# Moving what TensorE waits for ahead in the queues at each change of stage of the first batch

## The chip, the core and the metric

The kernel runs on one core of a Trainium2 chip. The core has TensorE (PE, matrix products into PSUM), VectorE (DVE), ScalarE (ACT), GpSimd (POOL) and SyncE (SP), which here issues the transfers. Each engine works through its own instructions in the order of the program, and waits at an instruction until what it needs is there. The metric is the time of one execution on the device in microseconds (us), a median of several.

## The reference

There are two blocks. The first is a long convolution by Fourier transform over 12480 positions, for 4 batches and 128 channels, with a filter that a small network makes from embeddings of the positions. The second is a gated layer over all 49920 tokens.

```python
h_filt = (np.maximum(pos_emb @ w1, 0.0) @ w2) * np.exp(-0.01 * pos)[:, None]
u = x * v
y = irfft(rfft(u, n=2 * S, axis=1) * rfft(h_filt, n=2 * S, axis=0), n=2 * S, axis=1)[:, :S, :]
a = (x * y).reshape(B * S, D)          # B, S, D = 4, 12480, 128
h = a @ w_in                           # w_in 128 x 2048
out = (h * np.cos(h)) @ w_out          # w_out 2048 x 128
```

## The kernel before

The transform is done in two steps of 96 and 120 points, as matrix products. The stages of the first batch have the names F1 (first step forward), F2 (second step forward, and the product with the filter's spectrum), I1 (first step back) and I2 (second step back). The filter goes through its own F1 just ahead of the first batch's F1, and F2 takes the filter and the first batch together (`f2_both_units`). With I2 the gated layer begins, and the later batches run between its matmuls until the end.

The program is written with generators: one `next` puts a small piece of work into the queues. `units` runs a stage: `before` puts in what a unit needs, `mm` its matmuls, `after` what empties its PSUM banks, one unit later. Beside F1 and I1 other work is strewn in by `beside`: the conversion of the gated layer's weights, which arrive as 64-bit numbers, in eight pieces a matrix (`convert_units`), and six groups of twiddled rows for I2 (`some_groups`). There are eight PSUM banks in these stages. A tile of a pool with `bufs=2` shares two buffers with its namesakes: a third one gets its buffer when all that uses the first one is done, its store too.

```python
    def convert_units(pool, pieces):
        raws, half = [], None
        for i in range(len(pieces) + 1):
            while len(raws) < min(i + 2, len(pieces)):
                raws.append(pool.tile([P, WCOL, 2], U32, name="raw", bufs=3))
                nc.sync.dma_start(raws[-1][:, :, :], pieces[len(raws) - 1][1])
            yield
            if i > 0:
                float32_join(pieces[i - 1][0], raws[i - 1], *half)
            if i < len(pieces):
                half = float32_parts(pool, raws[i])
...  # class Tables, def sines: for each output, one multiply-add chain on the engine, then:
                self.waiting.append((dst, t, TWO_PI / turn))
                yield
                if len(self.waiting) == self.lag:
                    self.finish(1)
        def finish(self, n):
            for _ in range(n):
                dst, t, scale = self.waiting.pop(0)
                nc.scalar.activation(dst, t, AF.Sin, scale=scale)
...  # def inverse_tables, after ten such outputs, with lag 4, on GpSimd:
        t.finish(len(t.waiting))
        for kept, made in ((csd, cs), (rowsd, rows), (twd, tw_t)):
            nc.sync.dma_start(kept[:, :, :], made[:, :, :])
...  # def turn, called by make_w for w and by make_t for tm:
        nc.scalar.activation(term, first, AF.Copy, scale=one)
        if spare is None:
            nc.vector.scalar_tensor_tensor(out=dst, in0=second, scalar=other, in1=term,
                                           op0=ALU.mult, op1=ALU.add)
        else:
            nc.scalar.activation(spare, second, AF.Copy, scale=other)
            nc.gpsimd.tensor_tensor(dst, term, spare, op=ALU.add)
...
    def f1_evict(ps, b, share):
        copy, negated = f1_takers(b, share)
        pj = ps[:, 0:4 * N1].rearrange("p (i r k) -> p r k i", i=2, r=2)
        copy(out=parts[0:ODD, :, :, b, :], in_=pj[0:ODD])
        yield
        copy(out=parts[ODD:KE, 0, :, b, :], in_=pj[ODD:KE, 1])
        negated(parts[ODD:KE, 1, :, b, :], pj[ODD:KE, 0])
        yield
...
    def f2_product(pool, ps, h, k1, whole):
        y = parts[0:N2, :, k1:k1 + 2, :, :].rearrange("p r k b i -> p r b (k i)")
        t = pool.tile([N2, 2, CB, 4], F32, name="t", bufs=1 + whole)
        uu = ps[0:N2, :].rearrange("p (r b j) -> p r b j", r=2, j=4)
        if whole:
            for r, (dst, hh) in enumerate(((y, h[:, :, :, :]), (t[:, :, :, :], h[:, ::-1, :, :]))):
                u = uu[:, r]
                twice = bass.AP(tensor=u.tensor, offset=u.offset,
                                ap=[u.ap[0], [0, 2], *u.ap[1:]])
                nc.vector.tensor_tensor(dst, twice, hh, op=ALU.mult)
                yield
        for r, op in ((0, ALU.subtract), (1, ALU.add)):
            if not whole:
                nc.vector.tensor_tensor(y[:, r], uu[:, 0], h[:, r], op=ALU.mult)
                yield
                nc.vector.tensor_tensor(t[:, r], uu[:, 1], h[:, 1 - r], op=ALU.mult)
            nc.gpsimd.tensor_tensor(y[:, r], y[:, r], t[:, r], op=op)
            yield
...
    def i1_evict(pool, ps, b):
        pj = ps[0:N1, 0:4 * N2].rearrange("p (i r j) -> p r j i", i=2, r=2)
        other = pool.tile([N1, N2, 2], F32, name="other")
        nc.scalar.copy(out=other[:, :, :], in_=pj[:, 1])
        for h, op in ((0, ALU.add), (1, ALU.subtract)):
            nc.vector.tensor_tensor(slots[0:N1, b, h * N2:(h + 1) * N2, :], pj[:, 0],
                                    other[:, :, :], op=op)
            yield
...
    def units(n, steps, before, mm, after, parts, ahead=2):
        for j in range(min(ahead, n)):
            for _ in before(j) or ():
                pass
        yield 0.0
        last = iter(())
        for j in range(n):
            early = iter(before(j + ahead) or () if j + ahead < n else ())
            now = None
            for i in range(parts):
                if i == 0 or 2 * i == max(parts, 2):
                    now = mm(j, now, min(i, 1))
                if i == 0 and parts == 1:
                    now = mm(j, now, 1)
                next(last, None)
                next(early, None)
                yield steps / parts
            for _ in early:
                pass
            next(last, None)
            last = after(j, now)
        for _ in last:
            pass
        yield REST
...
    def f2_both_units(bank):
        with tc.tile_pool(name="both", bufs=2) as pool:
            ws = {}
            def before(j):
                ws[j] = pool.tile([KE, 2, N2], F32, name="w")
                for i in range(2):
                    make_w(ws[j][:, i, :], 2 * j + i, half=bank)
                nc.sync.dma_start(wd[j, :, :, :], ws[j][:, :, :])
            def mm(j, ps, i):
                if i == 0:
                    ps = bank(), bank()
                for filt in range(2):
                    f2_mm(ps[filt], ws[j], 2 * j, i, filt=filt == 1)
                return ps
            def after(j, ps):
                h = pool.tile([N2, 2, CB, 4], F32, name="h", bufs=3)
                nc.scalar.activation(h[:, :, :, :].rearrange("p r b j -> p (r b j)"),
                                     ps[1][0:N2, :], AF.Copy, scale=1.0 / M)
                nc.sync.dma_start(hd[j, :, :, :, :], h[:, :, :, :])
                yield from f2_product(pool, ps[0], h, 2 * j, True)
            yield from units(N1 // 2, F2_STEPS, before, mm, after, 4, ahead=1)
...
    def some_groups(pool):
        for g in SOME:
            t = pool.tile([N1, G, 2, R], F32, name="some", bufs=2)
            yield from make_group(pool, g, t, G, bufs=2)
        next(backs[0])
...  # the main program
            f1 = f1_units(bank, ftile[0:FR, :, :, :], 0.53, f1_evict_filter)
            for _ in first_u:
                for _ in range(2):
                    next(f1)
            keep.__exit__(None, None, None)
            with tc.tile_pool(name="tables", bufs=1) as pool:
                sines = inverse_tables(pool)
                for i, _ in enumerate(f1):
                    if i % 5 == 0:
                        next(sines, None)
                for _ in sines:
                    pass
            backs = [inverse_units(lambda: bank(), b) for b in range(B)]
            def beside(units, pieces, more=lambda pool: iter(())):
                with tc.tile_pool(name="convert", bufs=1) as pool:
                    convert, other = convert_units(pool, pieces), more(pool)
                    for i, _ in enumerate(units):
                        if i % 14 == 0:
                            next(convert, None)
                        elif i % 5 == 0:
                            next(other, None)
                    for _ in [*convert, *other]:
                        pass
            beside(f1_units(bank, slots[0:R, :, :, :], 0.55),
                   [(wind[:, c], w) for c, w in in_pieces])
            lpool = ctx.enter_context(tc.tile_pool(name="late", bufs=1))
            cs = third_table(lpool)
            nc.sync.dma_start(cs[:, :, :], csd[:, :, :])
            for _ in f2_both_units(bank):
                pass
            first.close()
...
            w_in_sb = wpool.tile([D, DFF], F32, name="w_in_sb")
            w_out_sb = wpool.tile([P, NFC, D], F32, name="w_out_sb")
            quarter = wpool.tile([P, 1], F32, name="quarter")
            nc.vector.memset(quarter[:, :], 0.25)
            nc.sync.dma_start(w_in_sb[:, :], wind[:, :])
            beside(i1_units(bank), [(w_out_sb[:, c, :], w) for c, w in out_pieces], some_groups)
```

## Time and profile before

The three runs took 3785.52, 3782.50 and 3784.62 us, median 3784.62 us. The profiled execution has a span of 3782.9 us. Times of stretches and of single instructions count from the start of that span.

| engine | busy us | share of the span |
|---|---|---|
| TensorE matmuls (PE) | 3701.9 | 98% |
| TensorE weight loads (PEld) | 2107.3 | 56% |
| VectorE (DVE) | 2762.4 | 73% |
| GpSimd (POOL) | 2592.6 | 69% |
| ScalarE (ACT) | 2520.3 | 67% |

The stages that the change touches lie in the first 350 us:

| stage of the first batch | first matmul at us | last matmul begins, or group ends, at us |
|---|---|---|
| F1 of the filter | 63.2 | 112.7 |
| F1 | 112.7 | 164.8 |
| F2 | 169.5 | 267.7 |
| I1 | 271.0 | 331.7 |
| I2 | 336.6 | into the gated layer |

How to read the lines below: `L404` is line 404 of the kernel; `ps<-c,slots` gives the tiles written and read; `x14` is a number of instructions. An idle time has behind `<-` the engine, tile and line whose end is thought to have ended it. A matmul of 32-bit numbers stands as two instructions. The granted clock is TensorE's, as a share of full speed. In the chain, each step is followed back to what released it.

### The profile page before, as it was taken

The numbers are of one execution on the slowest core, as the hardware profiler recorded it, in microseconds if no ns is written. First come the engines' busy times: TensorE is split into PE (matmuls) and PEld (weight loads), VectorE is DVE, ScalarE is ACT, GpSimd is POOL, SyncE is SP. The second block draws the span as 40 slices with busy tenths as digits, with TensorE's granted clock in tenths as the row PEclk, the third lists the DMA queues.
The fourth block names the chain that finished last, engine by engine and source line by source line (L and its number), as shares of the span: only waits on it lengthen the run. The fifth ranks groups of instructions, "written<-read, shape, count | busy, mean of one in ns | idle before, by whom it ended". The sixth has DMA issues, their size and how long they took to land.

```text
span 3782.9 us, 47199 instructions
## 1 busy us (share of the span) xinstructions
PE 3701.9 (98%) x13546; PEld 2107.3 (56%) x13546; DVE 2762.4 (73%) x5562; ACT 2520.3 (67%) x4683; POOL 2592.6 (69%) x2342
## 2 busy tenths in 40 slices
PE   7898999999999999999999999999999999999999
PEld 6777555655466555555565556555566544444444
DVE  7887887688866777778766786788765566666666
ACT  5756776766665557666665567666664677777777
POOL 7667886588854665688745664788644577777776
PEclk9999999999999999999999999999999999999999
DMA  5263552022202650122103540122105200000000
GB/s 166 69 179 106 149 147 57 18 70 79 74 18 67 179 159 27 33 78 78 57 18 110 173 127 18 51 78 76 41 12 167 87 20 20 17 21 20 17 22 13
DMA packets 209498, 276.14 MB, mean 73 GB/s; under 512 B 17111, under 2 KB 146535, under 8 KB 209111
## 3 DMA queue, kind: packets, MB, share of 16 engines
q1 hardware_dynamic: 209239, 273.12, 24.7%
q8 instruction: 109, 1.79, 0.2%
q14 instruction: 150, 1.23, 0.1%
HBM read 193.64 MB, written 79.42 MB: 72 GB/s over the span
## 4 chain that ended last, share of the span: by engine, by line
PE 83%; POOL 6%; DVE 3%; DMA 3%; ACT 2%; issue 2%; SPq 0%; POOLq 0%; DVEq 0%; ACTq 0%
PE ph L737 32%; PE acc L762 27%; PE cv L762 5%; PE cv L501 4%; PE cv L476 4%; POOL f L746 4%; PE cv L404 3%; PE cv L445 3%; PE ph L126 2%; DMA hd<-h 2%; PE ps L404 1%; POOL tm L297 1%; DMA tm<-td 1%; DVE k L743 1%; ACT cs L751 1%
## 5 line engine op out<-in xcount | busy, mean ns | idle before, releaser
L746 POOL TENSOR_TENSOR f<-a,k 128x512 f32<-128x512 f32 (+1 forms) x1568 | 1987.4, 1268 | 1054.2 <-DVE k L743 1052.0
L737 PE MATMUL ph<-at,w_in_sb 128*128 128x512 f32 (+1 forms) x3136 | 1600.2, 592 | 5.8 <-DVE gt L753 5.2
L740 ACT ACTIVATE a<-ph,quarter 128x512 f32<-128x512 f32 (+1 forms) x1568 | 1073.4, 685 | 760.5 <-PE ph L737 751.0
L762 PE MATMUL acc<-gt,w_out_sb 128*128 128x512 f32 (+1 forms) x2688 | 1374.1, 593 | 9.7 <-ACT ot L768 9.3
L753 DVE TENSOR_TENSOR gt<-ph,cs 128x512 f32<-128x512 f32 (+1 forms) x1568 | 1077.3, 687 | 318.5 <-ACT cs L751 288.9
L743 DVE TENSOR_SCALAR k<-a 128x512 f32<-128x512 f32 (+1 forms) x1568 | 768.5, 490 | 623.4 <-ACT a L740 601.6
L751 ACT ACTIVATE cs<-f 128x512 f32<-128x512 f32 (+1 forms) x1568 | 980.3, 625 | 330.6 <-POOL f L746 328.1
L762 PEld LDWEIGHTS acc<-gt,w_out_sb 128*128 128x128 f32 x2688 | 505.6, 189 | 662.8 <-issue 619.5
L737 PEld LDWEIGHTS ph<-at,w_in_sb 128*128 128x128 f32 x3136 | 554.0, 190 | 338.7 <-issue 269.5
L471 POOL TENSOR_TENSOR slots<-slots,t 120x256 f32<-120x256 f32 x384 | 311.4, 817 | 58.7 <-DVE t L464 26.0
L501 PEld LDWEIGHTS cv<-slots,tm 96*104 96x104 f32 x1920 | 241.0, 171 | 110.7 <-issue 83.0
L501 PE MATMUL cv<-slots,tm 96*104 96x128 f32 x1920 | 255.6, 275 | 10.4 <-DVE tm L293 4.9
L762 PE MATMUL cv<-gt,w_out_sb 128*128 128x512 f32 (+1 forms) x448 | 224.5, 583 | 0.7 <-DVE gt L753 0.7
L476 PEld LDWEIGHTS cv<-cs,slots 120*96 120x96 f32 x1536 | 176.7, 167 | 67.6 <-issue 65.7
L476 PE MATMUL cv<-cs,slots 120*96 120x120 f32 x1536 | 183.1, 266 | 0.0
L445 PE MATMUL cv<-slots,w 124*120 124x256 f32 x576 | 173.0, 380 | 0.0
L445 PEld LDWEIGHTS cv<-slots,w 124*120 124x120 f32 x576 | 103.6, 184 | 123.8 <-issue 111.1
L404 PEld LDWEIGHTS cv<-c,slots 104*124 104x124 f32 x768 | 132.5, 192 | 71.2 <-issue 58.3
L404 PE MATMUL cv<-c,slots 104*124 104x192 f32 x768 | 151.2, 326 | 4.8 <-DVE gt L753 3.5
L762 PEld LDWEIGHTS cv<-gt,w_out_sb 128*128 128x128 f32 x448 | 84.9, 190 | 104.5 <-issue 99.5
L392 DVE TENSOR_TENSOR xt<-xt,vt 104x256 f32<-104x256 f32 x177 | 138.3, 788 | 0.4 <-DMA vt<-in_v_dram 0.4
L486 DVE TENSOR_TENSOR slots<-cv,other 96x240 f32<-96x240 f32 x384 | 133.7, 394 | 4.2 <-ACT other L484 4.2
(129 smaller groups left out, 2564.1 us busy)
## 6 DMA issues: line engine op xcount, KB each, us to landing
h<-hd SPq DMA_DIRECT2D x144, 240.0 KB
tm<-td SPq DMA_DIRECT2D x96, 312.0 KB
xt<-in_x_dram SPq DMA_DIRECT2D x120, 208.0 KB
vt<-in_v_dram SPq DMA_DIRECT2D x120, 208.0 KB
xs<-in_x_dram SPq DMA_DIRECT2D x120, 208.0 KB
zd<-zs SPq DMA_DIRECT2D x119, 208.0 KB
zb<-zd SPq DMA_DIRECT2D x96, 256.0 KB
w<-wd SPq DMA_DIRECT2D x144, 116.2 KB
```

The costliest lines, as they stand in the source:

```text
L404: nc.tensor.matmul(ps[0:KE, i * 2 * N1:(i + 1) * 2 * N1], u[:, b, 0:KE, i], c1[0:u.shape[0], :, :].rearrange("p r k -> p (r k)"), start=Tr ...
L445: nc.tensor.matmul(pi, w[:, i, :], parts[0:KE, :, k], start=True, stop=True)
L471: nc.gpsimd.tensor_tensor(y[:, r], y[:, r], t[:, r], op=op)
L476: nc.tensor.matmul(ps[0:N1, (i * 2 + r) * N2:(i * 2 + r + 1) * N2], parts[0:N2, r, :, b, i], cs[:, r, :], start=True, stop=True)
L501: nc.tensor.matmul(ps[0:R, i * D:(i + 1) * D], t[:, i, r, :], slots[0:N1, :, place, :], start=(r == 0), stop=(r == 1))
L737: nc.tensor.matmul(ph[:, 0:m], w_in_sb[:, c * P:(c + 1) * P], ats[n][:, 0:m], start=True, stop=True)
L740: nc.scalar.activation(a[:, 0:m], ph[:, 0:m], AF.Identity, bias=quarter[:, 0:1], scale=INV_TWO_PI)
L743: nc.vector.tensor_scalar(out=k[:, 0:m], in0=a[:, 0:m], scalar1=ROUND, scalar2=ROUND, op0=ALU.add, op1=ALU.subtract)
L746: nc.gpsimd.tensor_tensor(f[:, 0:m], a[:, 0:m], k[:, 0:m], op=ALU.subtract)
L751: nc.scalar.activation(cs[:, 0:m], f[:, 0:m], AF.Sin, scale=TWO_PI)
L753: nc.vector.tensor_tensor(gt[:, 0:m], ph[:, 0:m], cs[:, 0:m], op=ALU.mult)
L762: nc.tensor.matmul(accs[n][:, 0:m], w_out_sb[:, c, :], gt[:, 0:m], start=(c == 0), stop=(c == NFC - 1))
```

## The change

At each change of stage of the first batch, what TensorE waits for is put ahead in the queues:

- tables: the last four sines no longer come as one block; they are strewn one by one between the evictions, and the first batch's F1 starts among them;
- first matrices: the first pair of twiddled matrices `w` of F2 is made at the start of F1 and not after it; its pool moves out of F2's pool for that, and the stores of `w` now come after the store of `h` of the unit, those of the first ones after the first `h`;
- last sums: the two last sums of F2's product go to VectorE in place of GpSimd;
- conversions: the pieces come every 11th step in F1 and every 10th in I1 (before: every 14th), the groups for I2 at every fourth step (before: every fifth);
- transfers and groups: the first group of I2 with its transfers is put in ahead of the last group of `some_groups`, not after everything.

No arithmetic is added or left out.

```diff
--- before.py
+++ after.py
@@ -1,5 +1,6 @@
 import math
 from contextlib import ExitStack
+from itertools import chain
 
 import concourse.bass as bass
 import concourse.tile as tile
@@ -265,7 +266,9 @@
                            [(rows[:, i, :], q) for i, q in enumerate((0, 1, 2, 3))])
         yield from t.sines(mid, part4, TURN, [(tw_t[:, 0, :], 1), (tw_t[:, 1, :], 0)],
                            eighths=slice(H - 1, N2, H))
-        t.finish(len(t.waiting))
+        while t.waiting:
+            t.finish(1)
+            yield
         for kept, made in ((csd, cs), (rowsd, rows), (twd, tw_t)):
             nc.sync.dma_start(kept[:, :, :], made[:, :, :])
 
@@ -450,7 +453,7 @@
             for r, src in enumerate((ftile[0:KE, :, k, :], above[0:KE, :, k - KF, :])):
                 nc.tensor.matmul(pi[:, r], w[:, i, :], src, start=True, stop=True)
 
-    def f2_product(pool, ps, h, k1, whole):
+    def f2_product(pool, ps, h, k1, whole, sums=nc.gpsimd):
 
 
         y = parts[0:N2, :, k1:k1 + 2, :, :].rearrange("p r k b i -> p r b (k i)")
@@ -468,7 +471,7 @@
                 nc.vector.tensor_tensor(y[:, r], uu[:, 0], h[:, r], op=ALU.mult)
                 yield
                 nc.vector.tensor_tensor(t[:, r], uu[:, 1], h[:, 1 - r], op=ALU.mult)
-            nc.gpsimd.tensor_tensor(y[:, r], y[:, r], t[:, r], op=op)
+            sums.tensor_tensor(y[:, r], y[:, r], t[:, r], op=op)
             yield
 
     def i1_mm(ps, b, i):
@@ -601,32 +604,38 @@
             yield from units(N1 // 2, F2_STEPS, before, mm,
                              lambda j, ps: f2_product(pool, ps, hs.pop(j), 2 * j, False), 4)
 
-    def f2_both_units(bank):
-
+    def f2_both_units(bank, w_pool):
+
+        ws, unkept = {}, []
+
+        def before(j):
+            ws[j] = w_pool.tile([KE, 2, N2], F32, name="w")
+            for i in range(2):
+                make_w(ws[j][:, i, :], 2 * j + i, half=bank)
+            unkept.append(j)
+
+        def mm(j, ps, i):
+            if i == 0:
+                ps = bank(), bank()
+            for filt in range(2):
+                f2_mm(ps[filt], ws[j], 2 * j, i, filt=filt == 1)
+            return ps
+
+        def after(j, ps):
+            h = pool.tile([N2, 2, CB, 4], F32, name="h", bufs=3)
+            nc.scalar.activation(h[:, :, :, :].rearrange("p r b j -> p (r b j)"),
+                                 ps[1][0:N2, :], AF.Copy, scale=1.0 / M)
+            nc.sync.dma_start(hd[j, :, :, :, :], h[:, :, :, :])
+            while unkept:
+                k = unkept.pop(0)
+                nc.sync.dma_start(wd[k, :, :, :], ws[k][:, :, :])
+            yield from f2_product(pool, ps[0], h, 2 * j, True,
+                                  nc.vector if 2 * j + 2 == N1 else nc.gpsimd)
+
+        steps = units(N1 // 2, F2_STEPS, before, mm, after, 4, ahead=1)
+        yield next(steps)
         with tc.tile_pool(name="both", bufs=2) as pool:
-            ws = {}
-
-            def before(j):
-                ws[j] = pool.tile([KE, 2, N2], F32, name="w")
-                for i in range(2):
-                    make_w(ws[j][:, i, :], 2 * j + i, half=bank)
-                nc.sync.dma_start(wd[j, :, :, :], ws[j][:, :, :])
-
-            def mm(j, ps, i):
-                if i == 0:
-                    ps = bank(), bank()
-                for filt in range(2):
-                    f2_mm(ps[filt], ws[j], 2 * j, i, filt=filt == 1)
-                return ps
-
-            def after(j, ps):
-                h = pool.tile([N2, 2, CB, 4], F32, name="h", bufs=3)
-                nc.scalar.activation(h[:, :, :, :].rearrange("p r b j -> p (r b j)"),
-                                     ps[1][0:N2, :], AF.Copy, scale=1.0 / M)
-                nc.sync.dma_start(hd[j, :, :, :, :], h[:, :, :, :])
-                yield from f2_product(pool, ps[0], h, 2 * j, True)
-
-            yield from units(N1 // 2, F2_STEPS, before, mm, after, 4, ahead=1)
+            yield from steps
 
     def i1_units(bank):
         with tc.tile_pool(name="mid", bufs=2) as pool:
@@ -654,7 +663,8 @@
         for g in SOME:
             t = pool.tile([N1, G, 2, R], F32, name="some", bufs=2)
             yield from make_group(pool, g, t, G, bufs=2)
-        next(backs[0])
+            if g == SOME[-2]:
+                next(backs[0])
 
     def i2_units(bank, b, bufs):
 
@@ -857,33 +867,34 @@
             keep.__exit__(None, None, None)
             with tc.tile_pool(name="tables", bufs=1) as pool:
                 sines = inverse_tables(pool)
-                for i, _ in enumerate(f1):
-                    if i % 5 == 0:
-                        next(sines, None)
-                for _ in sines:
-                    pass
+                first_f1 = f1_units(bank, slots[0:R, :, :, :], 0.55)
+                for i, _ in enumerate(chain(f1, first_f1)):
+                    if i % 5 == 0 and next(sines, "made") == "made":
+                        break
 
 
 
             backs = [inverse_units(lambda: bank(), b) for b in range(B)]
 
-            def beside(units, pieces, more=lambda pool: iter(())):
+            def beside(units, pieces, every, more=lambda pool: iter(())):
                 with tc.tile_pool(name="convert", bufs=1) as pool:
                     convert, other = convert_units(pool, pieces), more(pool)
                     for i, _ in enumerate(units):
-                        if i % 14 == 0:
+                        if i % every == 0:
                             next(convert, None)
-                        elif i % 5 == 0:
+                        elif i % 4 == 1:
                             next(other, None)
                     for _ in [*convert, *other]:
                         pass
 
-            beside(f1_units(bank, slots[0:R, :, :, :], 0.55),
-                   [(wind[:, c], w) for c, w in in_pieces])
+            w_pool = first.enter_context(tc.tile_pool(name="w", bufs=2, side="right"))
+            f2 = f2_both_units(bank, w_pool)
+            next(f2)
+            beside(first_f1, [(wind[:, c], w) for c, w in in_pieces], 11)
             lpool = ctx.enter_context(tc.tile_pool(name="late", bufs=1))
             cs = third_table(lpool)
             nc.sync.dma_start(cs[:, :, :], csd[:, :, :])
-            for _ in f2_both_units(bank):
+            for _ in f2:
                 pass
             first.close()
 
@@ -898,7 +909,7 @@
             quarter = wpool.tile([P, 1], F32, name="quarter")
             nc.vector.memset(quarter[:, :], 0.25)
             nc.sync.dma_start(w_in_sb[:, :], wind[:, :])
-            beside(i1_units(bank), [(w_out_sb[:, c, :], w) for c, w in out_pieces], some_groups)
+            beside(i1_units(bank), [(w_out_sb[:, c, :], w) for c, w in out_pieces], 10, some_groups)
 
         ps_acc = ctx.enter_context(tc.tile_pool(name="ps_acc", bufs=1, space=PSUM))
         ps_h = ctx.enter_context(tc.tile_pool(name="ps_h", bufs=4, space=PSUM))
```

## The prediction

> **What bounds the kernel now.** I read the engines' shares first, then the waits of TensorE, then the stretches of the first 350 us one by one, and last the queues of the other engines around each gap. TensorE is busy for 98% of the span, so a microsecond counts only if TensorE is idle in it, or runs at the halved clock. The list of what TensorE waited for (line, releaser, us in total, times, longest) has these among its entries:
>
> ```profile
> PE ps L404 <- ACT slots L412: 8.1, 4, 7.1
> PE ps L404 <- DVE ftile L361: 6.3, 1, 6.3
> PE ps L445 <- DVE w L293: 6.4, 4, 4.7
> PE cv L501 <- DVE tm L293: 4.9, 1, 4.9
> PE ps L476 <- DVE slots L486: 4.4, 5, 1.4
> PE ps L476 <- POOL slots L471: 3.6, 2, 3.4
> ```
>
> Four of them are changes of stage of the first batch that the change touches: 7.1 us (filter's F1 to the first batch's F1), 4.7 (F1 to F2), 3.4 (F2 to I1), 4.9 (I1 to I2). Together 20.1 us, 0.53% of 3784.62 us. The 6.3 us at L361 is not touched. A second cost comes on top. In this table of stretches (length, then PE, PEld, DVE, ACT, POOL busy, granted clock, DMA share, GB/s) the clock after each gap stands at one half:
>
> ```profile
> 121.00:125.00 4.00, 4.00 (x14) 4.00 (x14) 1.19 (x3) 1.88 (x8) 0.00 (x0) 0.50 0.66 188
> 169.50:173.00 3.50, 3.50 (x9) 2.67 (x10) 0.68 (x3) 0.88 (x4) 0.00 (x0) 0.51 0.23 66
> 271.00:276.00 5.00, 4.73 (x27) 4.54 (x28) 1.50 (x5) 1.57 (x5) 1.16 (x3) 0.66 0.50 130
> 336.50:347.00 10.50, 9.83 (x39) 8.65 (x40) 2.32 (x6) 4.20 (x10) 3.38 (x5) 0.50 0.62 175
> ```
>
> At half clock 14 matmuls take 4 us, at full clock 20 take 3 us. So each gap costs up to 1.7 to 3 us more, if the matmuls behind it are TensorE's own limit and not that of the engines that empty PSUM.
>
> The removable sum looks like 20 us plus some 8 of clock. I expect much less, because at each of these places another queue is nearly as late. The evidence is ScalarE's queue before the first gap and before the second (start, length, instruction, count, idle before it and its releaser):
>
> ```profile
> 113.85 0.29 ACT L226 ACTIVATE rows<-turned 96x104 f32<-96x104 f32 x1 [1.73 <-POOL turned L217]
> 116.92 0.30 ACT L226 ACTIVATE tw_t<-turned 96x120 f32<-96x120 f32 x1 [2.78 <-POOL turned L217]
> 119.11 0.30 ACT L226 ACTIVATE tw_t<-turned 96x120 f32<-96x120 f32 x1 [1.89 <-POOL turned L217]
> ...
> 168.38 0.33 ACT L412 ACTIVATE slots<-ps 60x192 f32<-60x192 f32 x1
> 168.60 1.77 ACT L291 ACTIVATE ps<-even,tw_w 124x120 f32<-124x120 f32 x6
> ```
>
> The tables' last sines wait for GpSimd, which works without a pause until 119.1; two evictions stand behind them. And the last matmul of F1 is over at 164.8, yet ScalarE is still emptying banks until 168.7: F2 needs every channel of F1. Of the 4.7 us only the last 0.8 (168.7 to 169.5) is the making of `w`; 3.9 is backlog.
>
> **What the skill says.** The Trainium skill's page "TensorE: Matmul & The Clock Gate", section "What's actually happening", states that the clock is halved after an idle window of about 3.4 us and full again after such a window of work. The trace agrees on the size: the slow stretches above last 3.5 to 10.5 us, and a gap of 3.4 us was enough. The page "PSUM — Partial Sum Buffer", section "Engine vs sequencer instructions", says that the queues of ScalarE, VectorE and GpSimd are strictly first in, first out; the two evictions behind the sines agree. The page "GPSIMD Engine Reference", section 3.1 "Elementwise — side-by-side cycle accounting", gives about 2.6 cycles an element for a two-input operation against 1 on VectorE; here a sum of 120x256 takes 0.73 us on GpSimd, and VectorE's sum of 104x256 takes 0.41 us when alone and 0.9 beside GpSimd. The page "DMA: Bandwidth & Descriptors", section "Anatomy of one DMA", has a fixed part of about 2 us, mostly the receipt of the write (on the GpSimd path); the 116 KB store of `w` took 3.30 us in the chain below, from SyncE's queue.
>
> **Part 1, tables.** The four `Sin` that came in one block now come one or two at a time, five half-channels apart, and the first batch's F1 begins before they are over. GpSimd's end at 119.1 does not move. ScalarE's idle time from 111.8 on was 1.73 + 2.78 + 1.89 before the sines, then 0.56 + 1.53 + 0.49 waiting for the late TensorE, and 1.35 once for VectorE: 10.3 us. With one eviction of 1.15 us between the sines the waits become 1.7, about 1.6 and 0.7: 4.0. So ScalarE's chain of evictions gets 6.3 us ahead. The first `w` now sits inside it (two activations, 0.6): 5.7.
>
> **Part 2, conversions every 11th half-channel, not every 14th.** Nothing is removed; eight pieces move forward so that the end is free of them. In a period of 5.5 channels ScalarE has 3.0 channels at 1.05 and 0.8 for the piece, 4.0 us; VectorE about the same (2.5 at 1.23 and 0.9); GpSimd 0.85 + 1.08 + 1.08 + 0.73, with its gaps 3.9. TensorE needs 5.5 x 0.66 = 3.6. All three helpers are at their limit together, and each waits for another at the hand-over (ScalarE for the first mask, VectorE for the buffer whose store is under way). I charge 0.15 us a piece, 1.3 us. Left of part 1: 4.4.
>
> **Part 3, first `w` early.** The 0.8 us from the last eviction to the first matmul of F2 becomes about 0.1: 0.7. F2 then starts 4.4 + 0.7, rounded 5.0 us, earlier, near 164.5. The gap is still about 3 us, so whether the clock stays full is open.
>
> **Part 4, the stores of F2.** This is the step that I expect to take something back. F2 runs at about 2.02 us a pair of frequencies and not at the 1.74 of its eight matmuls, because `w` has two buffers: made, stored, and only then free for the pair after next. The chain of the span shows such stores beside those of `h`:
>
> ```profile
> 177.41 3.30 DMA wd<-w
> ...
> 202.29 3.59 DMA hd<-h
> 205.88 0.02 issue
> 205.92 0.04 issue
> 205.97 0.49 ACT h L624
> 206.46 4.10 DMA hd<-h
> ```
>
> `h`'s store stands behind the next `w`'s store in SyncE's queue and so leaves about 2 us after `h` is made. Turning the order round frees `h`, but the loop of `w` stays: 0.6 to make it, 3.3 to store it, 0.1 to go on, 4.0 us for two pairs. No gain per pair. At the start there is a loss: the store of the first `w` now comes only after the first `h`, and the third `w` needs the first one's buffer. Counted from the first matmul of F2: 1.9 us for the pair (3.5 at half clock), 0.4 for `h`, 0.4 to issue its store, 3.1 for the store of the first `w`, 0.7 for the third `w`. Its own store leaves at 6.5 us (8.2 at half clock) against 173.85 - 169.50 = 4.35 before. Every later pair is shifted by that: 2.2 us, or 3.9. I take 2.8.
>
> **Part 5, last sums on VectorE.** The chain at the end of F2 was: a wait of `h` of 0.45 us for a store (gone with the new order), two products, two sums on GpSimd at 0.73. On VectorE behind its own products the two sums take about 0.4 each and need no hand-over. First matmul at full supply of I1: 0.45 + 2 x 0.33 + 0.1 = 1.2 us earlier. The gap of 3.4 falls to some 2.2.
>
> **Part 6, I1 and the first group of I2.** The last join of a weight piece and the first `tm` leave the end of the stage (0.33 + 0.35 + 0.2 on VectorE); the pieces come every 5 channels instead of every 7, and the other groups every second instead of every 2.5. VectorE needs two additions of 0.33 a channel, 0.8 a piece, and waits 1.1 for ScalarE at each piece. That sum does not change by moving, and VectorE, not TensorE, was last here: TensorE ended at 331.7 and VectorE at 336.1. So of 4.9 us only about 1.2 go. For the clock in I1 and I2 together I add 0.9, because one of the two gaps should get short enough.
>
> **Sum.** -5.0 + 2.8 - 1.2 - 1.2 - 0.9 = -5.5 us, so 3784.6 - 5.5 = 3779.1. The remaining 3430 us run the same instructions in the same order, on a TensorE without pauses, so what is gained at the first group of I2 is kept.
>
> **Rivals.** First, all gaps close: TensorE starts each stage when the one before ends. That would be 20.1 us and several more of clock, 3758 to 3763. For it speaks that each gap has one named releaser; against it that ScalarE ends F1's evictions 3.9 us after TensorE and VectorE ends I1's 4.4 us after it, and both have only part of that idle before. Second, the start of F2 is worse than I think and the conversions jam: a cold start there, GpSimd at 5.5 of 5.4 us a period in I1 (3.7 for a piece, 2.5 groups at 0.62, hand-overs), its backlog passed on to ScalarE through the two spare buffers. That takes another 5 to 8 us: 3784 to 3787. For it speaks GpSimd's high load in both stages; against it that GpSimd has slack of about 2 us at each piece. Third, F2 itself gets faster: if `h`'s store was the true limit, the pairs fall from 2.02 towards 1.74 us, up to 40 x 0.28 = 11 us, 3768. For it speaks the chain, which names `h`'s store at every second pair; against it that `w`'s loop comes to the same 4.0 us.
>
> **Range and chances.** 3770 to 3786: the lower end is half of the third rival's gain or half of the first's on top of mine, the upper end the second rival. No path leads to 2% (75.7 us), since all that the change can remove is under 1%, and what it adds is a few waits of some us: faster 0.005, same 0.99, slower 0.005.
>
> **What would show each step.** F1: ScalarE's waits at L226 shrink, but do not vanish; F2 starts 3 to 7 us earlier, with a gap of 2 to 4 us before it. F2: a new wait of 2 to 4 us before its third pair, released by VectorE's `w`, and 2.0 us a pair afterwards. I1 starts 1 us sooner after F2's last matmul; I1 to I2 is still a gap of 3 us or more. I am wrong if F2 has no such wait or runs under 1.9 us a pair, if the gaps before F2 and I2 close, or if the time of I1 from its first to its last matmul changes by over 3 us.

## The result and the profile after

The changed kernel takes 3797.68 us (median of 4 runs, 3794.85 to 3800.33); the kernel before, beside it, 3783.56 (3782.23 to 3785.52). The ratio is 1.0037, with a 95% interval of 1.0019 to 1.0054: slower by 14 us, within 2%. Predicted were 3779.1 us and a gain.

The profiled execution has a span of 3794.5 us against 3782.9. In this table a stage counts from its first matmul; the gap is the time from its end to the next stage's first matmul.

| us | before | after | difference | predicted |
|---|---|---|---|---|
| F1 of the first batch and the gap behind it | 56.75 | 57.10 | +0.35 | -5.0 |
| F2 | 98.17 | 104.46 | +6.29 | +2.8 |
| gap from F2 to I1 | 3.37 | 2.67 | -0.70 | -1.2 |
| I1 | 60.66 | 71.99 | +11.33 | 0 |
| gap from I1 to I2 | 4.88 | 1.34 | -3.54 | -1.2 |
| from I2's first matmul to the 401st matmul of the gated layer with `w_in` | 480.82 | 475.50 | -5.32 | -0.9, with I1 |

The rows add up to 8.4 us; the spans differ by 11.6. Of the rest 1.7 us lie ahead of the first row: F1 starts at 114.45 us and not at 112.75. Kernels below with the old code up to there start F1 at 113.07 to 114.33, so this is not put down to the change. The last 1.5 lie behind the last row.

What TensorE waits for between 100 and 360 us in the changed kernel (line, releaser, us in total, times, longest):

```profile
PE ps L479 <- DVE slots L489: 10.9, 7, 2.7
PE ps L407 <- ACT slots L415: 7.5, 7, 3.8
PE ps L448 <- DVE w L296: 6.1, 8, 3.1
PE ps L448 <- ACT slots L415: 2.9, 1, 2.9
PE ps L479 <- POOL slots L474: 2.7, 1, 2.7
PE cv L504 <- DVE slots L489: 1.3, 1, 1.3
```

The long waits at the changes of stage are gone or shorter: 7.1 became 3.8, 4.7 became 2.9, 3.4 became 2.7, 4.9 became 1.3. That is the change's purpose, and it was reached. In their place stand waits inside the stages: in I1 (L479, before L476) 10.9 us for VectorE's evictions where there were 4.4, and a new one of 3.1 us at the third pair of F2.

The stretches of the changed kernel (length, then PE, PEld, DVE, ACT, POOL busy, granted clock, DMA share, GB/s) at F1's start, inside F2, inside I1 and at I2's start:

```profile
118.00:122.00 4.00, 1.02 (x4) 0.51 (x3) 1.63 (x6) 2.60 (x10) 2.35 (x6) 0.51 0.01 3
122.00:128.50 6.50, 5.73 (x18) 5.38 (x19) 2.81 (x9) 2.73 (x9) 0.00 (x0) 0.51 0.44 136
179.50:183.00 3.50, 2.98 (x7) 2.38 (x8) 3.46 (x8) 0.65 (x2) 1.37 (x2) 0.51 0.41 118
326.50:330.00 3.50, 3.50 (x21) 3.50 (x20) 2.37 (x8) 1.92 (x7) 2.55 (x5) 0.54 0.32 79
352.00:362.00 10.00, 9.10 (x55) 6.87 (x56) 3.80 (x9) 5.39 (x12) 4.34 (x5) 1.00 0.31 88
```

I2 now begins at full clock: 55 matmuls in 10 us where there were 39 in 10.5. That is the one place where the change pays, but the 5.3 us of the table overstate it. In seven kernels below with the same gap of 4.88 us before I2, the half clock lasts 3.9 to 5.9 us from I2's first matmul and not 10.5, and the 401st of those matmuls comes 476.2 to 479.3 us after it. The median of these and the kernel before is 478.5, so the closed gap is worth some 3 us behind I2's start. F1's start has a half clock for 10 us instead of 7 (of four kernels below with the old code in F1, three show 10 and one 7), and F2 and I1 have stretches of it that they did not have.

**F1.** TensorE's and ScalarE's queues at the start of the first batch's F1 (start, length, instructions, count, idle before and its releaser):

```profile
114.45 0.81 PE L407 MATMUL ps<-c,slots 104*124 104x192 f32 x4
117.05 1.97 PE L407 MATMUL ps<-c,slots 104*124 104x192 f32 x8 [1.79 <-ACT slots L415]
122.77 7.47 PE L407 MATMUL ps<-c,slots 104*124 104x192 f32 x27 [3.75 <-ACT slots L415]
...
120.81 0.30 ACT L227 ACTIVATE tw_t<-turned 96x120 f32<-96x120 f32 x1 [0.73 <-POOL turned L218]
121.13 0.47 ACT L423 COPY slots<-ps 64x384 f32<-64x384 f32 x1
121.51 0.64 ACT L294 ACTIVATE ps<-even,tw_w 124x120 f32<-124x120 f32 x2
122.18 0.31 ACT L425 COPY slots<-ps 60x192 f32<-60x192 f32 x1
```

One wait of 7.1 us has become two, 1.79 and 3.75. The eviction that TensorE needs at 122.77 has the last sine ahead of it, and in its midst the two activations of the early `w`.

**F2.** VectorE, TensorE and SyncE's transfers at its start:

```profile
171.78 0.62 DVE L296 SCALAR_TENSOR_TENSOR w<-even,tw_w,ps 124x120 f32<-124x120 f32 x2 [1.47 <-ACT ps L294]
179.54 0.59 DVE L296 SCALAR_TENSOR_TENSOR w<-even,tw_w,ps 124x120 f32<-124x120 f32 x2 [7.13 <-DMA wd<-w]
...
180.02 1.18 PE L448 MATMUL ps<-slots,w 124*120 124x256 f32 x2 [3.07 <-DVE w L296]
...
174.95 0.34 SPq L628 DMA_DIRECT2D hd<-h  x1
175.33 5.06 SPq L631 DMA_DIRECT2D wd<-w  x3
180.44 0.35 SPq L628 DMA_DIRECT2D hd<-h  x1
```

In the kernel before, SyncE's first stores of `w`:

```profile
169.67 4.42 SPq L613 DMA_DIRECT2D wd<-w  x3
```

The first `w` is on its way to memory only at 175.3, 3.8 us after F2's first matmul (before: 169.67, 0.2 us after it). The third `w` needs its buffer, and VectorE stands for 7.13 us.

**I1.** VectorE's groups from I1's first matmul to I2's first (line, shapes, count; busy, mean ns; idle before and its releaser), first in the kernel before, then in the changed one:

```profile
L486 DVE TENSOR_TENSOR slots<-ps,other 96x240 f32<-96x240 f32 x128 | 42.6, 396 | 14.6 <-ACT other L484 14.5
L133 DVE TENSOR_SCALAR power<-raw 128x256 uint32<-128x256 uint32 x8 | 3.4, 424 | 0.0
L151 DVE SCALAR_TENSOR_TENSOR power<-raw,power 128x256 uint32<-128x256 uint32 x8 | 3.3, 412 | 0.0
L141 DVE TENSOR_SCALAR sig<-raw 128x256 uint32<-128x256 uint32 x8 | 2.3, 284 | 0.0
```

```profile
L489 DVE TENSOR_TENSOR slots<-ps,other 96x240 f32<-96x240 f32 x128 | 42.7, 395 | 18.6 <-ACT other L487 17.8
L142 DVE TENSOR_SCALAR sig<-raw 128x256 uint32<-128x256 uint32 x8 | 5.6, 699 | 0.0
L152 DVE SCALAR_TENSOR_TENSOR power<-raw,power 128x256 uint32<-128x256 uint32 x8 | 4.0, 496 | 0.0
L134 DVE TENSOR_SCALAR power<-raw 128x256 uint32<-128x256 uint32 x8 | 2.5, 317 | 0.2 <-DMA raw<-in_moe_w_out_dram 0.2
```

The work is the same, and two things have grown. One is VectorE's share of the conversions: two masks and a join for each piece. The mask into `sig` (L142) takes 699 ns on average and not 284, the join (L152) 496 and not 412, while the mask into `power` (L134) fell from 424 to 317; together they grew from 9.0 to 12.1 us. The averages hide single slow masks: in the changed kernel three of the eight of L142 take 1.39 us and the other five 0.28. The kernel before has one such among the eight of L133:

```profile
300.00 1.40 DVE L133 TENSOR_SCALAR power<-raw 128x256 uint32<-128x256 uint32 x1
```

The other is VectorE's wait for ScalarE's half of the evictions, 17.8 us and not 14.5. Three places in the queues of the changed kernel show both:

```profile
282.86 0.47 ACT L294 ACTIVATE some<-rows,tw_t 96x208 f32<-96x208 f32 x1 [6.21 <-DMA tw_t<-twd]
...
296.44 2.37 POOL L300 TENSOR_TENSOR some<-some,spare 96x208 f32<-96x208 f32 x3
298.76 0.72 POOL L157 TENSOR_TENSOR w_out_sb<-sig,power 128x256 f32<-128x256 f32 x1
...
298.04 0.28 DVE L134 TENSOR_SCALAR power<-raw 128x256 uint32<-128x256 uint32 x1
298.24 1.39 DVE L142 TENSOR_SCALAR sig<-raw 128x256 uint32<-128x256 uint32 x1
...
299.66 0.42 ACT L145 ACTIVATE sig<-sig 128x256 f32<-128x256 uint32 x1 [2.10 <-DVE sig L142]
...
333.35 0.47 ACT L299 ACTIVATE spare<-rows,tw_t 96x208 f32<-96x208 f32 x1 [1.38 <-POOL tm L300]
...
334.81 2.60 DVE L489 TENSOR_TENSOR slots<-ps,other 96x240 f32<-96x240 f32 x8 [3.01 <-ACT other L487]
...
335.67 15.00 PE L479 MATMUL ps<-cs,slots 120*96 120x120 f32 x128 [2.69 <-DVE slots L489]
```

At I1's start the first activation of a group stands at the head of ScalarE's queue and waits for the load of `tw_t` until 282.86, 4.2 us after I1's first matmul, with all evictions behind it. At 298.24 VectorE's mask begins while GpSimd has one two-input operation after another, from 296.44 to 299.48; the mask takes 1.39 us in place of 0.28, and ScalarE waits 2.10 us for it. The other two slow masks, and the one in the kernel before, look the same: each began in the midst of a GpSimd operation and ended 0.15 us after the next one. The Trainium skill's page "SBUF — State Buffer", section "SBUF: two separate sides", says that VectorE and GpSimd share a pair of ports which one of them holds for a whole instruction while the other is fully blocked; for a VectorE instruction with one input, like the mask, it says so only of the modes that use both ports, and no run shows the mask's mode. The trace agrees in part only: the mask at 298.04, of the same shape, took 0.28 us in the midst of the same GpSimd operation. So the ports are a likely cause of the slow masks, not a shown one.

The third place is the first group of I2. Its activations stand among ScalarE's evictions, and one of them waits 1.38 us for GpSimd; VectorE then waits 3.01 us for ScalarE, and TensorE 2.69 us for VectorE, its longest wait in I1.

Of the 11.3 us in I1, 6.3 are TensorE standing still (10.9 us in place of 4.6). The other 5.1 are its 512 matmuls, busy for 61.1 us in place of 56.0: the mean granted clock in I1 is 0.91 in place of 0.97.

### The profile page after: what moved, and what is told of

The parts are those of the page before. It is cut to its first block, busy times and chain, and to the rows that moved or that the text cites. A ratio compares the mean times of both kernels' runs of the same rounds, so it can differ in the third digit from the quotient of the medians.

```text
span 3794.5 us, 47211 instructions
## 1 busy us (share of the span) xinstructions
PE 3706.3 (98%) x13546; PEld 2109.3 (56%) x13546; DVE 2767.9 (73%) x5564; ACT 2520.6 (66%) x4683; POOL 2591.0 (68%) x2340
## 3 DMA queue, kind: packets, MB, share of 16 engines
q8 instruction: 109, 1.79, 0.2%
## 4 chain that ended last, share of the span: by engine, by line
PE 82%; POOL 5%; DVE 3%; DMA 2%; ACT 2%; issue 1%; POOLq 0%; DVEq 0%; SPq 0%; ACTq 0%
PE ph L747 31%; PE acc L772 27%; PE cv L772 5%; PE cv L504 4%; PE cv L479 4%; POOL f L756 3%; PE cv L407 3%; PE cv L448 3%; PE ph L127 2%; DMA tm<-td 1%; PE ps L448 1%; POOL tm L300 1%; ACT cs L761 1%; DMA wd<-w 1%; DVE k L753 1%
## 5 line engine op out<-in xcount | busy, mean ns | idle before, releaser
L474 POOL TENSOR_TENSOR slots<-slots,t 120x256 f32<-120x256 f32 x382 | 309.5, 816 | 68.1 <-DVE t L467 29.1
L479 PEld LDWEIGHTS cv<-cs,slots 120*96 120x96 f32 x1536 | 176.7, 167 | 67.6 <-issue 65.7
L479 PE MATMUL cv<-cs,slots 120*96 120x120 f32 x1536 | 183.1, 266 | 0.0
```

The lines of the kernel that those rows point to most:

```text
L474: sums.tensor_tensor(y[:, r], y[:, r], t[:, r], op=op)
L479: nc.tensor.matmul(ps[0:N1, (i * 2 + r) * N2:(i * 2 + r + 1) * N2], parts[0:N2, r, :, b, i], cs[:, r, :], start=True, stop=True)
```

## The experiments

My theory after this reading: most of the loss is the density of conversions and groups in I1, then F2's start, where the third `w` waits for the first one's store; F1 gains nothing, because TensorE waits for a bank at half clock. Each part was undone alone in the changed kernel, then done alone in the kernel before. Times are medians; "ratio" is to runs of the kernel before beside them on the same chip, with its 95% interval. The medians of the kernel before were 3783.45 to 3784.59 us there, and differences in time to it are to the one beside. The stage columns are those of the first table, from one profiled execution each. The kernels with the same code up to F2 as the kernel before show 56.5 to 57.8 us for F1, so about 1 us there is noise.

| kernel | us | ratio | F1 | F2 | gap | I1 | gap |
|---|---|---|---|---|---|---|---|
| before | 3783.56 | | 56.75 | 98.17 | 3.37 | 60.66 | 4.88 |
| after | 3797.68 | 1.0037 (1.0019 to 1.0054) | 57.10 | 104.46 | 2.67 | 71.99 | 1.34 |
| after, old densities | 3791.14 | 1.0019 (1.0010 to 1.0027) | 55.88 | 105.51 | 2.69 | 64.43 | 3.77 |
| after, first store early | 3791.48 | 1.0023 (1.0015 to 1.0031) | 56.54 | 101.85 | 2.66 | 73.65 | 1.33 |
| after, groups later | 3795.12 | 1.0030 (1.0018 to 1.0042) | 56.56 | 106.67 | 2.67 | 69.08 | 2.94 |
| after, late `w`, old stores | 3786.94 | 1.0008 (1.0000 to 1.0017) | 54.95 | 97.88 | 2.68 | 72.04 | 1.33 |
| before, `h` stored first | 3791.58 | 1.0019 (1.0012 to 1.0026) | 57.08 | 104.45 | 3.02 | 60.65 | 4.88 |
| before, dense | 3790.01 | 1.0015 (1.0008 to 1.0022) | 58.79 | 98.80 | 3.06 | 68.14 | 2.66 |
| before, strewn tables | 3780.97 | 0.9992 (0.9984 to 1.0001) | 54.55 | 98.29 | 3.06 | 60.76 | 4.88 |
| before, first group and sums | 3785.90 | 1.0004 (0.9996 to 1.0013) | 57.80 | 98.44 | 2.69 | 64.73 | 4.23 |
| tables and last sums | 3780.76 | 0.9992 (0.9984 to 1.0000) | 55.13 | 99.27 | 2.69 | 60.96 | 4.88 |
| before, dense groups | 3786.11 | 1.0005 (0.9997 to 1.0013) | 56.54 | 98.02 | 3.06 | 63.31 | 3.28 |
| tables, sums, early `w` | 3782.46 | 0.9996 (0.9988 to 1.0005) | 55.70 | 98.78 | 2.70 | 60.50 | 4.88 |
| tables, sums, share 0.52 | 3784.30 | 1.0002 (0.9993 to 1.0010) | 55.59 | 98.86 | 2.70 | 61.10 | 4.88 |
| before, dense conversions | 3795.17 | 1.0028 (1.0018 to 1.0037) | 57.36 | 98.28 | 3.05 | 62.88 | 11.04 |
| after, three parts undone | 3782.61 | 0.9996 (0.9987 to 1.0004) | 54.31 | 98.17 | 2.70 | 63.86 | 4.36 |
| tables, sums, `w` at 60 | 3780.68 | 0.9992 (0.9984 to 1.0001) | 54.13 | 99.66 | 2.70 | 61.37 | 4.88 |
| the same, share 0.52 | 3782.49 | 0.9996 (0.9987 to 1.0004) | 54.60 | 99.27 | 2.70 | 60.99 | 4.88 |

### Parts undone in the changed kernel

**Old densities.**

```diff
-                        if i % every == 0:
+                        if i % 14 == 0:
-                        elif i % 4 == 1:
+                        elif i % 5 == 0:
```

> The changed kernel with both densities as before: a conversion at every 14th half-channel, a step of the groups at every fifth; all else of the change stays. My theory (the dense steps of I1 overload VectorE and GpSimd, which share, and so TensorE waits for VectorE's evictions): I1 falls from 72.0 us to 61 to 64, the gap from I1 to I2 grows back from 1.3 to 2.5 to 5 us, F2 stays at 104 to 105; the kernel takes about 3790, 6 to 9 us less than the changed one. Rival (I1 is longer because its start waits for the load of tw_t and because its clock starts at one half): I1 stays at 69 us or more and the time is the changed kernel's within 2 us.

I1 fell to 64.4 us, the gap grew to 3.8, and 6.5 us of the 14.1 are gone. The density is a cause, and the rival falls. But 3.8 us more than before stay in I1: another part of the change sits there too.

**First store early.**

```diff
-            unkept.append(j)
+            if j == 0:
+                nc.sync.dma_start(wd[j, :, :, :], ws[j][:, :, :])
+            else:
+                unkept.append(j)
```

> The changed kernel, but the store of the first w leaves as soon as it is made, during F1; from the second w on h goes first. My theory (the third pair waits for the first w's store, which stands behind the first h): the wait of TensorE at the third pair falls from 3.1 us to under 0.5, F2 takes 98 to 100 us instead of 104.5, I1 stays at 72; the kernel takes about 3792. Rival (F2 is longer because the turned order makes each pair wait for a store): F2 stays over 103 us.

Half a hit. TensorE's wait at the third pair is gone, but one of 1.76 us stands at the fourth, since the second `w` is still stored behind the first `h`:

```profile
177.55 0.59 DVE L296 SCALAR_TENSOR_TENSOR w<-even,tw_w,ps 124x120 f32<-124x120 f32 x2 [3.18 <-DMA wd<-w]
```

F2 takes 101.9 us, outside both expectations. The order costs at each of the first buffers, not at the first alone. After that a pair takes 2.0 us, as before.

**Groups later**, so that nothing at I1's start waits for `tw_t`.

```diff
-                        elif i % 4 == 1:
+                        elif i % 4 == 1 and i > 16:
```

> The changed kernel, but the groups of I2 made beside I1 begin only after its 16th half-channel, so that no activation that waits for the load of tw_t stands in ScalarE's queue at I1's start. My theory: the first eviction on VectorE comes 2.5 us after I1's first matmul instead of 5.3, and I1 takes 68 to 70 us instead of 72; most of its loss (8 us) stays, as the density does. Rival (the blocked queue at the start is the whole loss): I1 falls to 61 to 63. The kernel takes 3793 to 3796, by the rival 3787.

I1 took 69.1 us, 2.9 less, VectorE evicted 2.2 us after I1's first matmul, and the gap to I2 took 1.6 back. The mask kept its 699 ns. The blocked queue is the smaller part of I1's loss.

**Late `w`, old order of stores.**

```diff
-            w_pool = first.enter_context(tc.tile_pool(name="w", bufs=2, side="right"))
-            f2 = f2_both_units(bank, w_pool)
-            next(f2)
             ...
-            for _ in f2:
+            for _ in f2_both_units(bank):   # as before: w made, stored, then h
```

> The changed kernel, but the first w is made after F1 and the stores of w stand ahead of those of h, both as before; the last sums stay on VectorE. My theory (early w brings nothing since F2 waits for ScalarE's last evictions): the gap from F1 to F2 grows by 0.5 to 1 us, F2 takes 98 to 99 us instead of 104.5, in all about 5 us less, 3792 to 3793. Rival (the early w is what holds F1 up, its activations standing between evictions while the clock is low): F2's first matmul comes 2 us or more earlier, and the kernel takes 3790 or less.

This gave back the most, 10.7 us. F2 is at 97.9 us, as expected, and the rest came unexpectedly in F1: F2's first matmul lies 54.95 us after F1's first instead of 57.10. The gap behind F1 did grow, from 2.93 to 3.69 us, but F1 itself shrank by 2.9. TensorE at F1's start:

```profile
116.62 1.57 PE L407 MATMUL ps<-c,slots 104*124 104x192 f32 x8 [1.79 <-ACT slots L415]
119.70 10.54 PE L407 MATMUL ps<-c,slots 104*124 104x192 f32 x47 [1.50 <-ACT slots L415]
```

The wait of 3.75 us is one of 1.50. The rival was right: the early `w` held F1 up. The other runs agree: the five kernels with `w` at F1's start take 55.70 to 57.10 us for F1 with its gap, the seven with the strewn tables and `w` elsewhere 54.13 to 55.59.

### Parts done alone in the kernel before

**`h` stored first.**

```diff
-                nc.sync.dma_start(wd[j, :, :, :], ws[j][:, :, :])
+                unkept.append(j)
...
                 nc.sync.dma_start(hd[j, :, :, :, :], h[:, :, :, :])
+                while unkept:
+                    k = unkept.pop(0)
+                    nc.sync.dma_start(wd[k, :, :, :], ws[k][:, :, :])
```

> The kernel before with one part of the change: the stores of h stand ahead of those of w. My theory: F2 has a new wait at its third pair and takes 2 to 6 us more than 98.2 us, then 2.01 us a pair as before; the kernel takes 3786 to 3790. Rival (w's store is late only because the first w is made early in the changed kernel): F2 takes 98 us as before, 3784.

F2 takes 104.45 us, 6.3 more, and the time is 7 us longer, both just over what was expected. That F2 agrees with the changed kernel to 0.01 us is chance: two other kernels with the turned order and the early `w` show 105.51 and 106.67. VectorE and TensorE at the third pair:

```profile
178.99 0.59 DVE L293 SCALAR_TENSOR_TENSOR w<-even,tw_w,ps 124x120 f32<-124x120 f32 x2 [7.89 <-DMA wd<-w]
...
179.48 0.67 PE L445 MATMUL ps<-slots,w 124*120 124x256 f32 x2 [3.68 <-DVE w L293]
```

The turned order alone makes most of F2's loss. Counted from F2's first matmul, the tenth `h` begins to be made at 25.18 us here, 20.41 in the kernel before and 26.36 in the changed kernel: 4.8 of the 6.0 us that the start loses there come without the early `w`. Further on, this run has one more wait of 1.46 us for a store of `w`, at 238 us. So about 1 us of the changed kernel's loss may belong to the early `w`.

**Dense.**

```diff
-                        if i % 14 == 0:
+                        if i % every == 0:          # 11 in F1, 10 in I1
-                        elif i % 5 == 0:
+                        elif i % 4 == 1:
```

> The kernel before with one part of the change: conversions at every 11th half-channel of F1 and every 10th of I1, groups at every fourth. My theory: I1 grows from 60.7 to 68 to 72 us, the gap from I1 to I2 falls from 4.9 to about 3; the kernel takes 3789 to 3793. Rival (what is made earlier is missing later, so the sum stays): I1 grows, but the start of I2 stays within 2 us of 336.6 and the kernel takes 3784 to 3786.

I1 took 68.1 us, 7.5 more, the gap 2.2 less. F1 took 2.0 more (of which 1 may be noise). The rival falls: I2 starts some 5 us later in the sum of I1 and gap. VectorE's mask in I1:

```profile
L141 DVE TENSOR_SCALAR sig<-raw 128x256 uint32<-128x256 uint32 x8 | 5.6, 701 | 0.0
```

**Dense groups alone**, conversions at every 14th as before.

```diff
-                        elif i % 5 == 0:
+                        elif i % 4 == 1:
```

> The kernel before with a step of the groups at every fourth half-channel instead of every fifth, in I1; the conversions stay at every 14th. Theory A (what costs is VectorE and GpSimd working at once, when conversions are dense as well): I1 takes 61 to 63.5 us, against 68.1 with both dense; 3783 to 3786. Theory B (what costs is that the groups' first activation comes earlier and waits for tw_t with the evictions behind it, 5.7 us where the densities alone were changed): I1 takes 65 to 68 us; 3787 to 3790.

The first activation of a group does wait for the load (next line, from the groups of ScalarE in I1), even longer than in the changed kernel, and yet I1 takes only 63.3 us. Theory A.

```profile
L291 ACT ACTIVATE some<-rows,tw_t 96x208 f32<-96x208 f32 x24 | 11.2, 469 | 6.5 <-DMA tw_t<-twd 6.5
```

**Dense conversions alone.**

```diff
-                        if i % 14 == 0:
+                        if i % every == 0:          # 14 in F1, 10 in I1
                         elif i % 5 == 0:
```

> The kernel before with conversions at every 10th half-channel of I1 instead of every 14th; groups at every fifth. Theory A (only both together cost, since VectorE and GpSimd are then at work at the same instants): I1 takes 61 to 63 us and the mask on VectorE keeps its 284 ns; 3783 to 3786. Theory B (the dense conversions cost in themselves: ScalarE waits for each mask and VectorE for ScalarE): I1 takes 64 to 66 us; 3786 to 3789.

I1 took 62.9 us and the mask kept 283 ns, as theory A has it, but the time is far over both expectations. The edit did more than I meant: a half-channel whose number divides by 10 now goes to a conversion, and only 13 of 128 are left for the 24 steps of the groups (before: 24). The other 11 came in one block after I1, and I2 waited for them:

```profile
PE cv L501 <- DVE tm L293: 11.0, 1, 11.0
```

So the run shows that dense conversions with thin groups do not slow the mask, but it is no clean test of density. From these runs: dense groups +2.7 us in I1, both dense +7.5. With either alone all eight masks into `sig` take 0.28 us; three slow ones of eight come only with both.

**First group of I2 earlier, and last sums on VectorE.**

```diff
-        next(backs[0])                       # after all groups
+            if g == SOME[-2]:
+                next(backs[0])               # in the loop, before the last group
...
-            nc.gpsimd.tensor_tensor(y[:, r], y[:, r], t[:, r], op=op)
+            sums.tensor_tensor(y[:, r], y[:, r], t[:, r], op=op)   # VectorE for the last pair
```

> The kernel before with two small parts of the change: the first group of I2 begun one group earlier among I1's, and the last sums of F2 on VectorE. My theory: the gap from F2 to I1 is about 0.7 us shorter, that from I1 to I2 falls from 4.9 to 3 or less and TensorE's clock is then full at I2's start, which gave the changed kernel 5 us; the kernel takes 3777 to 3781. Rival (the gap closed only because the dense steps stretched I1): the gap stays at 4 us or more with the half clock behind it, 3782 to 3784.

A miss. The gap before I1 is 0.7 us shorter, but I1 is 4.1 us longer, and the gap to I2 stays at 4.2 with half clock behind it. Work put into I1 ahead of its end lengthened I1 and hardly shortened what follows. It is the first group that did it: with the sums and the tables alone (below) I1 takes 60.96 us. The trace shows the same pattern as in the changed kernel, VectorE waiting 1.98 us for ScalarE behind the group's activations, and TensorE 1.89 for VectorE. The rival was right that the gap does not close by this alone; its time was 1.9 us too low. Density alone does not close it either (2.66): it takes both.

**Strewn tables.**

```diff
-        t.finish(len(t.waiting))
+        while t.waiting:
+            t.finish(1)
+            yield
...
+                first_f1 = f1_units(bank, slots[0:R, :, :, :], 0.55)
-                for i, _ in enumerate(f1):
+                for i, _ in enumerate(chain(f1, first_f1)):
```

> The kernel before with one part of the change: the steps of the sine tables strewn over the filter's F1 and the first half-channels of the first batch's F1. My theory: ScalarE's waits for sines shrink to about 4 us and F1 of the first batch, from the filter's last matmul on, is 1 to 4 us shorter; F2 begins at 166 to 169 instead of 169.5; 3780 to 3783. Rival (TensorE then waits for banks behind the sines and its clock stays at one half for as long): F2 begins at 169 to 171, 3784 to 3785.

F1 with its gap is 2.2 us shorter and the time 3.6 us less in the medians (0.9984 to 1.0001: just not clear of no change). This is the only part for which a gain in time is likely.

### Combinations

**Tables and last sums on VectorE.** The edits are those above.

> The kernel before with two parts of the change: the strewn sine tables and the last sums of F2 on VectorE. My theory (these are the only two parts that help): F2 begins at 168 to 169, F2 takes 98 us, the gap from F2 to I1 is 2.7 instead of 3.4 us, I1 takes 61 to 63 (its first group waits longer for the load of tw_t, which eats the 0.7); the kernel takes 3779 to 3782. Rival (the 0.7 stays as it is and adds to the tables' 3.6): 3777 to 3779.5.

0.2 us under the tables alone, within the noise: the 0.37 us shorter gap is not seen in the time.

**With the early `w`, stores in the old order.**

```diff
+            w_pool = first.enter_context(tc.tile_pool(name="w", bufs=2, side="right"))
+            f2 = f2_both_units(bank, w_pool)      # its before() stores w at once
+            next(f2)
             beside(first_f1, ...)
```

> Strewn tables, last sums on VectorE, and the first w made during F1, but its store and all later ones ahead of h as before. Theory A (the early w's activations and its bank hold the evictions up while the clock is at one half): from the filter's last matmul to F2's first it takes 56 to 58 us against 54.7 with strewn tables alone, and F2 takes 97 to 98; 3781 to 3784. Theory B (only the turned order of stores costs, the early w itself gains): 53.5 to 54.5 us, 3777 to 3780.

55.54 us from the filter's last matmul to F2's first, between the two theories; the gap fell from 5.4 to 3.8, and F1 paid it back at its start:

```profile
121.21 9.03 PE L407 MATMUL ps<-c,slots 104*124 104x192 f32 x38 [3.31 <-ACT slots L415]
```

The time is 1.7 us above that of tables and sums, which the intervals of both allow as noise.

**With the first `w` at the 60th half-channel of F1 instead.**

```diff
+            def with_w(units):
+                for i, step in enumerate(units):
+                    if i == 60:
+                        next(f2)
+                    yield step
-            beside(first_f1, ...)
+            beside(with_w(first_f1), ...)
```

> Strewn tables, last sums on VectorE, stores in the old order, and the first w made at the 60th half-channel of F1. Theory A (it was the place that cost): no wait of 3.3 us at F1's start, F1 49 to 50 us, the gap from F1 to F2 3.8 instead of 5.4 us; from the filter's last matmul to F2's first 53 to 54 us instead of 54.7; 3778 to 3780. Theory B (ScalarE's backlog sets F2's start, and the two activations lengthen it wherever they stand): 54.5 to 55.5 us, 3780 to 3782.

The wait at F1's start is 1.50 us, F1 took 49.0 us and 54.0 us lie from the filter's last matmul to F2's first, as theory A has it. The gap, however, is 5.2 and not 3.8, released by ScalarE's last eviction: F1 ran ahead of ScalarE, and its backlog sets F2's start. The time, 3780.68, is that of the tables and sums without it.

**ScalarE's share 0.52 instead of 0.55**, with tables and sums, and in a second kernel with `w` at the 60th half-channel too.

```diff
-                first_f1 = f1_units(bank, slots[0:R, :, :, :], 0.55)
+                first_f1 = f1_units(bank, slots[0:R, :, :, :], 0.52)
```

> Strewn tables and last sums on VectorE, and ScalarE's share of the evictions of the first batch's F1 0.52 instead of 0.55 (33 channels of 64 instead of 35). Theory A (F2 waits for ScalarE's backlog, which VectorE, done 3.4 us earlier, could have taken): the gap from F1 to F2 falls from 5.4 to 3 to 4 us, F2 begins 1.5 to 2 us earlier; 3777 to 3780. Theory B (VectorE, which also makes the masks of the conversions, becomes the last): TensorE waits for VectorE's evictions within F1 and F2 begins no earlier; 3780 to 3783.

> As the run before it, and ScalarE's share of the evictions 0.52 instead of 0.55. Theory A (with w made, F2 waits for ScalarE's evictions alone, and VectorE can take two channels): the gap from F1 to F2 is 2 to 3 us; 3776 to 3779. Theory B (VectorE becomes the last, or TensorE waits for it within F1): no gain over the run before it, or a loss of 1 to 3 us.

Both were slower than without it, by 3.5 and 1.8 us. In the first, `w` waits for the store of the last converted piece (VectorE, next line):

```profile
169.46 1.09 DVE L296 SCALAR_TENSOR_TENSOR w<-even,tw_w,ps 124x120 f32<-124x120 f32 x4 [2.93 <-DMA wind<-power]
```

In the second that wait is gone, and TensorE still waits 3.8 us for ScalarE. Why ScalarE with two channels less ends no sooner was not followed further.

**The changed kernel without density, early `w` and turned stores.**

> The changed kernel without its dense steps, without the early w and without the turned order of stores: strewn tables, last sums on VectorE and the first group of I2 begun earlier are left. If the parts add up: the kernel before by -3.6 (tables) and +1.3 (the other two), 3781 to 3784, with I1 at 64 us, F2 at 98. Rival (the parts hang together, and the rest of the change costs as well): over 3786.

3782.61 us, I1 at 63.9, F2 at 98.2: the parts add up. Added from the single runs: 7.0 (order of stores), 5.4 (density), -3.6 (tables), 1.3 (first group and sums), 1.7 (early `w`: 3782.46 - 3780.76), together 11.8 us, against 14.1 measured; the intervals of the single runs, some 3 us to each side, are wide enough for the rest.

None of the versions beats the kernel before clearly. The three fastest, all with the strewn tables and without the costly parts, lie 0.08% below it, with intervals that end at 1.0000 or 1.0001.

## Why the prediction was wrong

The reading of the kernel before held: gaps with a second queue nearly as late behind each, so that little was to be had. The sign was wrong because parts that I counted as moved work cost time where they were moved to.

- **Part 6** failed most, at "That sum does not change by moving, and VectorE, not TensorE, was last here". If VectorE is last, every delay of VectorE is TensorE's, and the sum did change: the masks and joins by 3.1 us (9.0 to 12.1), VectorE's waits for ScalarE's `other` by 3.3. I1 grew by 11.3 us where I had 0: 7.5 for density alone, 4.1 for the first group. Three things are seen in it. ScalarE's queue is blocked at I1's start: with the groups later I1 takes 2.9 us less, the slow masks staying. There are two more slow masks than before, 1.1 us each of VectorE's time; no run takes them away without the rest, so their share of the 7.5 is not shown. And the first group's activations stand among the evictions. I had GpSimd's load in the second rival, "5.5 of 5.4 us a period in I1", but looked there for GpSimd's backlog and not for VectorE and ScalarE standing still. The rival's 5 to 8 us are near the 7.5, and I discounted it by "slack of about 2 us at each piece"; but the measured time lies 10 us above even that rival. I also predicted "I1 to I2 is still a gap of 3 us or more"; it closed to 1.3, and with it came some 3 us of clock, not 0.9.
- **Part 4** had the right mechanism and a mis-sized term. The wait at the third pair came (3.07 us, "2 to 4" predicted), and the pairs kept 2.0 us. But the cost is 6.3 us and not 2.8. The start was at half clock, for which the working itself gave 3.9, and I took a middle value; the third `w`'s own store had left by 180.39, 8.8 us after F2's start (8.2 worked out, 4.35 in the kernel before). Counted from F2's first matmul, the third `h` began to be made at 11.91 us and not 7.16: 4.75 of the 6.3. Of the other 1.5, 1.2 were lost in the sixth and seventh interval between two `h`, 2.68 and 2.53 us where the kernel before had 1.74 and 2.28; I had taken every later pair to be shifted and nothing more. The cause that I gave for the 2.0 us a pair, the loop of `w`, is not shown: in the second half of F2 TensorE itself is full (19.97 of 20 us from 230 to 250 in the kernel before). In the first half it stays open; neither a third buffer of `w` nor a fourth of `h` was tried. The third rival, that `h`'s store was the limit, is refuted: with `h` first a pair takes the same.
- **Part 1** was right on ScalarE's waits (1.72, 1.61 and 0.73 against 1.7, 1.6 and 0.7) and wrong in what they give: "ScalarE's chain of evictions gets 6.3 us ahead". Behind the sines ScalarE had nothing to empty, as TensorE stood for a bank and then ran at half clock until 128 us. By itself the part gives 2.2 us in the stage and 3.6 in the time, the latter not clear of the noise.
- **Part 2**, 1.3 us for the pieces in F1, was 2.0, about right within the noise.
- **Part 3** failed: the early `w` was to gain 0.7 us and cost 0.6 of ScalarE. It stood in the middle of the eviction that TensorE needed most, and cost 2.2 us net in the stage taken out of the changed kernel (57.10 against 54.95) and 0.6 put in beside tables and sums (55.70 against 55.13). I counted its two activations as work only, not as a delay of the eviction behind them, though the strict order of the queue was in my own text.
- **Part 5**, -1.2 us, gave 0.4 to 0.7 in the gap. In the time it is not seen.

## What to carry to other kernels

Putting work earlier in a queue is not free when the stage it moves into is bound by the engine that runs it, or by one that waits for it: count the delay of what stands behind, and look in the trace whether VectorE and GpSimd get their denser work at the same instants. Before turning the order of two transfers, follow which buffer each one frees, and what the engine that sets the pace does while it waits in the first rounds. Take such a change apart from the start: of the parts here one gained 3.6 us in the medians, and three (order of stores, density, early `w`) cost 14 when tried alone.

## What was not expected of the hardware

- VectorE's mask over 128x256 words, with one input from SBUF, took 0.28 us in most places, also where a GpSimd two-input operation began just after it (0.02 us, at 292.60 in the changed kernel). Three of eight took 1.39 us in the changed kernel and one 1.40 in the kernel before: each began in the midst of a GpSimd two-input operation with another behind it, and ended 0.15 us after the second. The one at 298.04 began in the midst of such an operation too and took 0.28; what sets them apart stays open.
- At I2's start the clock was full after gaps of 1.33 and 1.34 us, and at one half after gaps of 2.66 (for over 7 us), 2.94 (some 3) and 4.88 us (10.5 in the kernel before, 3.9 to 5.9 in seven others). So a gap shorter than the 3.4 us of the Trainium skill's page "TensorE: Matmul & The Clock Gate", section "What's actually happening", was enough to halve it; the stretches from 326.5 to 330 and 336.5 to 340 in I1 come with no wait over 2.7 us. Here the measurement decides over the simple reading of that figure that the prediction used.
